# The order of the output products in the second half of a spectral and mixture kernel: in whole tiles four steps behind, or in single matmuls by a schedule that is three steps behind at both ends

## The chip, the cores and the metric

The kernel runs on one core of one Trainium2 chip. The metric is the device time of one execution in microseconds. A core has five engines with a queue of instructions each: PE (TensorE, matmuls; its weight loads have a row of their own, PEld), DVE (VectorE), ACT (ScalarE), POOL (GpSimd) and SP (SyncE, which issues the DMAs here). Each queue is worked off in the order in which the program wrote it; engines wait for each other through semaphores.

## The reference

Three layers in a row: a layer in the frequency domain over x [8, 3072, 256], a soft mixture of experts, and a two-layer network with a softmax-weighted activation and a layer norm over 24,576 tokens. The second half of the kernel computes what follows from the logits of the mixture to the end; the last layer is

```python
def _moe2_ref(x, w_in, w_out, g_ln):
    h = x @ w_in
    e = np.exp(h - np.max(h, axis=-1, keepdims=True))
    sm = e / (np.sum(e, axis=-1, keepdims=True) + 1e-09)
    solu = h * sm
    mu = np.mean(solu, axis=-1, keepdims=True)
    var = np.mean((solu - mu) ** 2, axis=-1, keepdims=True)
    ln = (solu - mu) / np.sqrt(var + 1e-06) * g_ln
    return (ln @ w_out).astype(np.float32)
```

Here x is the mixture's output. The kernel has multiplied the mixture's 32 slots with w_in beforehand, so that one product of a tile of mixture weights gives h at once, and it has folded g_ln and the mean's subtraction into w_out.

## The kernel before

The first half (some 637 us) computes the frequency layer, the mixture's weights and the slots. The second half is the function phase2. It cuts the 24,576 tokens into NI = 192 tiles of 128 tokens and runs a software pipeline over them, written out by hand: the loop at L1309 has a step i for every tile and six more, and each step issues a different stage of several tiles. No scheduler changes the order; what a step writes first stands first in its engine's queue. For tile t the stages are:

- hmat (L1059), in step t-3, on PE: two matmuls of 512 columns give h of the tile in PSUM ("hps", three buffers; the buffer comes free when umul of tile t-3 is done).
- rowmax (L1074), in step t-2, on DVE; expo (L1080), in step t-2, on ACT; umul (L1088), in step t-1, on DVE, the product of h and exp ("u").
- In step t-1 also, the transposition of u. For most tiles it is blocks (L1112): a DVE transpose of 32x32 blocks and four DMAs that move the blocks to their places ("t2"). For every eighth tile (turned, L1100: t % 8 == 6 and t < 172) it is turn (L1148) instead: eight transposes on PE into the tile's own hps, copied out by ACT. For the last two tiles (direct, L1097: 190 and 191) it is trans (L1123) in step t, eight transposes on PE into "pu", and direct_parts (L1137), where ACT writes the rounded half of u, and DVE the rest, half a tile at a time and by turns.
- vari (L1193), in step t, on ACT: the sum of squares.
- uhi (L1165), in step t+2: the transposed u rounded to the fast matmul format ("uh"), three quarters by ACT and one by POOL. ulo (L1177), in step t+2: the remainder ("ul"), in two halves on POOL (for tiles 188 and 189 the second half on DVE). In every fourth step the four small POOL instructions of rstd (L1224) stand between the two halves of ul.
- prod (L1200), in step t+4: the output product, 24 matmuls of 256 columns into a half of a PSUM bank ("po2"; two tiles share a bank, there are two banks): 16 with uh, then 8 with ul. A turned tile has 4 in plain float32 and 12 others.
- outp (L1239): ACT scales two tiles of the product into "osb", in every odd step i, for tiles i-7 and i-6; this frees their PSUM bank. Stores follow on SP.

The products of one tile are split in two places around a turned tile T: in step T-1 the first 16 of tile T-5 stand before turn(T) and the other 8 behind it, and in step T the first 12 of tile T-4 stand before hmat(T+3). In the first four steps six dummy matmuls ("idle", run_on) follow hmat.

Of the kernel before, what the change touches and what calls it, by code (L numbers as in the profile page):

```python
# [8 lines left out]
F32 = mybir.dt.float32  # L9
# [26 lines left out]
def kernel(  # L36
# [26 lines left out]
    B, N, D = x.shape  # L63
# [5 lines left out]
    NI = T // 128  # L69
# [18 lines left out]
    def mm(out, lhsT, rhs, start=True, stop=True):  # L88
        PE.matmul(out=out, lhsT=lhsT, rhs=rhs, start=start, stop=stop)  # L89

    def tp(out, in_, k=128):
        PE.transpose(out=out, in_=in_, identity=ident[0:k, 0:k])  # L92
# [813 lines left out]
    def phase2(p2: ExitStack, pw: ExitStack):  # L906
# [3 lines left out]
        gw = k_p.tile([128, 8, 2, D], F32R, name="gw")  # L910
# [13 lines left out]
        p = ExitStack()  # L924
# [5 lines left out]
        ps = pt.tile([128, 2, 32], F32, name="pslt", tag="pt")  # L930
# [85 lines left out]
        for fh in range(2):  # L1016
            n = 0
# [13 lines left out]
        def right(name, bufs, **k):  # L1031
            return p2.enter_context(tc.tile_pool(name=name, bufs=bufs, side="right", **k))

        f_p = right("f_p", 1)
        gwf = f_p.tile([128, 4, D], F32, name="gwf")
# [7 lines left out]
        po_p = right("po_p", 2, space=PSUM)  # L1043
        NG = NI // 4
        ctt, hps, et, ut, uht, stt, osb, pot = {}, {}, {}, {}, {}, {}, {}, {}
# [51 lines left out]
        def direct(i):  # L1097
            return i >= NI - 2

        def turned(i):  # L1100
            return i % 8 == 6 and i < NI - 20
# [21 lines left out]
        def trans(i):  # L1123
            if i >= NI or not direct(i):
                return
            ps = ph_p.tile([128, 8, 128], F32, name="pu", tag="hps")
            for c in range(8):
                tp(ps[:, c, :], ut[i][:, 128 * c:128 * c + 128])
            ut[i, 0] = ps
# [67 lines left out]
            sq = e_p.tile([128, DFF], F32, name="sq", tag="sq", bufs=1)  # L1197
            ACT.activation(out=sq, in_=ut.pop(i), func=AF.Square, bias=st[:, 2, k:k + 1], scale=-float(DFF), accum_out=st[:, 3, k:k + 1])  # L1198

        def prod(i, left=0):  # L1200
            if i < 0 or i >= NI:
                return
            if i not in pr_ops:
                uh, ul = uht.pop(i)
                if i % 2 == 0:
                    pot[i // 2, 0] = po_p.tile([128, 2, D], F32, name="po2", tag="po2")
                ps = pot[i // 2, 0][:, i % 2, :]
                if turned(i):
                    ops = [(uh[:, f, :].bitcast(F32), gwf[:, f, :]) for f in range(4)]
                    hi = [(f, ul[:, f - 4, :], ul[:, f, :]) for f in range(4, 8)]  # L1210
                else:
                    ops = []
                    hi = [(f, uh[:, f, :], ul[:, f, :]) for f in range(8)]
                for f, h, _ in hi:
                    ops += [(h, gw[:, f, 0, :]), (h, gw[:, f, 1, :])]
                ops += [(l, gw[:, f, 0, :]) for f, _, l in hi]
                pot[i] = ps
                pr_ops[i] = [(ps, a, b, n == 0, n == len(ops) - 1) for n, (a, b) in enumerate(ops)]
            ops = pr_ops[i]
            while len(ops) > left:  # L1220
                mm(*ops.pop(0))


        def rstd(i):  # L1224
            if i >= NI:
                return
            j, k = divmod(i, 4)
            if k < 3:
                return
            st = stt[j]  # L1230
            k = slice(0, 4)
            POOL.tensor_scalar(out=st[:, 1, k], in0=st[:, 1, k], scalar1=1e-9, scalar2=(1e-6 * float(DFF) ** 3) ** 0.5, op0=ALU.add, op1=ALU.mult)
            POOL.tensor_tensor(out=st[:, 1, k], in0=st[:, 1, k], in1=st[:, 1, k], op=ALU.mult)
            POOL.tensor_tensor(out=st[:, 3, k], in0=st[:, 3, k], in1=st[:, 1, k], op=ALU.add)
            POOL.tensor_tensor(out=st[:, 4, k], in0=st[:, 3, k], in1=mhalf[:, k], op=ALU.pow)

        o_todo, pr_ops = {}, {}

        def outp(i):  # L1239
            if i < 0 or i >= NI:  # L1240
# [22 lines left out]
        def run_on(n):  # L1263
            ps = po_p.tile([128, 128], F32, name="idle", tag="po2")
            for _ in range(n):
                mm(ps, ones, ones)
# [42 lines left out]
        for i in range(NI + 6):  # L1309
            j, k = divmod(i, 4)  # L1310
            if turned(i):
                prod(i - 4, 12)
            hmat(i + 3)
            if i < 4:
                run_on(6)
            trans(i)
            rowmax(i + 2)
            umul(i + 1)
            blocks(i + 1)
            store(i - 6)  # L1320
            late_c(i)
            last_c(i)
            if i % 2 == 1:
                outp(i - 7)
                outp(i - 6)
            if turned(i):
                expo(i + 2)
                vari(i)
            else:
                vari(i)  # L1330
                expo(i + 2)
            direct_parts(i)
            if i <= NI + 1:
                uhi(i - 2)
                ulo(i - 2, 0)
            rstd(i)
            if i <= NI + 1:
                ulo(i - 2, 1)
            if k == 1:
                pieces(j + 2)  # L1340
            if turned(i + 1):
                prod(i - 4, 8)
                turn(i + 1)
            prod(i - 4)
        while o_todo:
            store(min(o_todo))

# [143 lines left out]
```

## Time and profile before

| what | value |
|---|---|
| device time, median of 3 runs | 1326.49 us (1325.54 to 1326.93) |
| the profiled execution's own time | 1324.1 us |
| its span, first to last instruction | 1322.3 us |
| granted TensorE clock, mean over the span | 0.995 |
| PE busy, 11,040 matmuls | 1264.3 us, 96% of the span |
| PEld busy | 1113.9 us, 84% |
| DVE busy | 1161.5 us, 88% |
| POOL busy | 1013.4 us, 77% |
| ACT busy | 988.7 us, 75% |
| chain that ended last: share of PE, and of the output products alone | 72%, 37% |

The page's shares are means over both halves. The second half starts at about 637 us and is much denser than the first: in it PE, DVE, ACT and POOL are all busy for more than nine tenths of the time. So its limit is read step by step from the timeline, and from the chain of waits that ended last, which goes back from the last instruction to what released it.

### The profile page before, as it was taken

The page shows a single profiled execution, that of the slowest core. Times are in us where ns is not written, and L with a number is a line of the kernel's source. Part 1 is how long each engine was busy: PE and PEld are TensorE (multiplying, and loading weights), DVE is VectorE, ACT ScalarE, POOL GpSimd, SP SyncE. Part 2 cuts the span into 40 slices and gives each one's busy share as a digit, 9 for nine tenths or more (in the row PEclk, how much of TensorE's full clock was granted, in tenths as well). Part 3 has the DMA queues.
Part 4 walks back from the last instruction along what each step waited for, and adds up shares of the span by engine and source line. Part 5 has one row for each costly group of instructions (what it writes and reads, how often), then busy time and mean ns, then how long its engine had stood idle before and what let it go on. Part 6 is the DMA issues. An engine that isn't in the chain of part 4 may idle for free.

```text
span 1322.3 us, 30973 instructions
## 1 busy us (share of the span) xinstructions
PE 1264.3 (96%) x11040; PEld 1113.9 (84%) x11040; DVE 1161.5 (88%) x1564; ACT 988.7 (75%) x1830; POOL 1013.4 (77%) x1112
## 2 busy tenths in 40 slices
PE   5989999999999999998799999999999999999998
PEld 2768878776787878875599999999999999999998
DVE  1868898989898989765899999999999999999995
ACT  3445556555565665544599999999999999999996
POOL 0769686776869584442398999999999989999995
PEclk8999999999999999999999999999999999999999
DMA  8986465463828374349567778777877787777874
GB/s 265 271 233 186 127 168 168 124 196 96 240 68 240 80 208 157 113 125 354 126 165 176 200 190 204 199 180 188 198 196 199 179 217 196 193 200 178 202 187 123
DMA packets 181338, 241.79 MB, mean 183 GB/s; under 512 B 21984, under 2 KB 137056, under 8 KB 181184
## 3 DMA queue, kind: packets, MB, share of 16 engines
q1 hardware_dynamic: 180736, 238.62, 67.0%
q8 instruction: 88, 1.44, 0.5%
q10 hardware_dynamic: 448, 1.18, 0.3%
q14 instruction: 66, 0.54, 0.1%
HBM read 92.00 MB, written 59.11 MB: 114 GB/s over the span
## 4 chain that ended last, share of the span: by engine, by line
PE 72%; DVE 11%; POOL 5%; DMA 5%; issue 3%; ACT 2%; SPq 1%; DVEq 0%; ACTq 0%; POOLq 0%
PE po L89 37%; PE pb L89 7%; PE pm L89 6%; PE hps L89 6%; PE xps L89 5%; PE s L89 4%; PE pa L89 3%; PE sps L92 2%; DVE st L1078 2%; DVE u L1093 2%; PE hps L92 2%; DMA t<-tb 1%; DMA xc<-in_x_dram 1%; POOL x L229 1%; POOL x L225 1%
## 5 line engine op out<-in xcount | busy, mean ns | idle before, releaser
L1188 POOL TENSOR_TENSOR ul<-t,uh 128x512 fp32r<-128x512 f32 x336 | 431.1, 1301 | 43.3 <-ACT uh L1174 42.7
L89 PEld LDWEIGHTS po<-gw,uh 128*128 128x128 f32 x2736 | 347.4, 188 | 14.0
L89 PE MATMUL po<-gw,uh 128*128 128x256 f32 x2736 | 353.7, 280 | 0.0
L1078 DVE TENSOR_REDUCE st<-hps 128x1 f32<-128x1024 f32 x192 | 229.1, 1194 | 10.5 <-PE hps L89 10.5
L1093 DVE SCALAR_TENSOR_TENSOR u<-hps,e 128x1024 f32<-128x1024 f32 x192 | 232.1, 1209 | 0.5 <-ACT e L1085 0.3
L89 PE MATMUL po<-gw,ul 128*128 128x256 f32 x1620 | 228.1, 284 | 0.0
L1085 ACT ACTIVATE e<-hps,st 128x1024 f32<-128x1024 f32 x192 | 215.5, 1123 | 16.5 <-DVE st L1078 16.4
L1198 ACT ACTIVATE sq<-u,st 128x1024 f32<-128x1024 f32 x192 | 223.0, 1162 | 0.3 <-DVE u L1093 0.3
L1116 DVE STREAM_TRANSPOSE tb<-u 128x1024 f32<-128x1024 f32 x169 | 210.5, 1245 | 5.9
L349 POOL TENSOR_TENSOR s<-yb,s 128x512 f32<-128x512 f32 x95 | 124.7, 1312 | 112.3 <-DVE s L348 107.2
L89 PEld LDWEIGHTS po<-gw,ul 128*128 128x128 f32 x1620 | 206.1, 188 | 1.1
L1174 ACT ACTIVATE uh<-t 128x768 fp32r<-128x768 f32 x169 | 143.4, 849 | 0.0
L89 PEld LDWEIGHTS xps<-d_sb,apt 128*128 128x128 f32 x768 | 94.9, 194 | 56.6 <-issue 31.5
L89 PE MATMUL xps<-d_sb,apt 128*128 128x128 f32 x768 | 111.0, 288 | 13.7 <-DMA apt<-ad 10.1
L89 PE MATMUL hps<-gst,ct 128*128 128x512 f32 x338 | 106.2, 396 | 7.6 <-DVE u L1093 6.1
L252 ACT ACTIVATE asb<-s 128x1024 f32<-128x1024 f32 x56 | 57.6, 1028 | 72.5 <-PE s L89 67.1
L309 POOL TENSOR_TENSOR sl<-xsum,sh 128x256 fp32r<-128x256 f32 x93 | 76.5, 822 | 35.5 <-ACT sh L308 35.4
L225 POOL TENSOR_TENSOR x<-xc 112x512 f32<-112x512 f32 x56 | 73.5, 1313 | 37.9 <-DMA xc<-in_x_dram 37.9
L293 DVE TENSOR_TENSOR xsum<-xps,xi 128x256 f32<-128x256 f32 x96 | 39.6, 413 | 54.0 <-ACT xh L292 38.8
L1249 ACT ACTIVATE osb<-po,st 128x256 f32<-128x256 f32 x192 | 80.3, 476 | 8.3 <-PE po L89 4.7
L348 DVE TENSOR_SCALAR s<-yb 128x512 f32<-128x512 f32 x95 | 77.4, 815 | 3.7
L229 POOL TENSOR_TENSOR x<-xc 112x512 f32<-112x512 f32 x56 | 78.9, 1410 | 0.0
(211 smaller groups left out, 2389.3 us busy)
## 6 DMA issues: line engine op xcount, KB each, us to landing
t<-tb SPq DMA_DIRECT2D x676, 128.0 KB, 2.8
xc<-in_x_dram SPq DMA_DIRECT2D x128, 192.0 KB, 3.9
apt<-ad SPq DMA_DIRECT2D x96, 256.0 KB, 4.0
out_dram<-osb SPq DMA_DIRECT2D x47, 512.0 KB, 3.8
ad<-asb SPq DMA_DIRECT2D x112, 192.0 KB, 3.7
ct<-c_dram SPq DMA_DIRECT2D x96, 128.0 KB, 4.1
wt<-in_moe_w_dram SPq DMA_DIRECT2D x21, 512.0 KB, 9.1
ws<-in_moe_w_dram SPq DMA_DIRECT2D x22, 256.0 KB, 6.4
```

What stands on the lines that cost most here:

```text
L89: PE.matmul(out=out, lhsT=lhsT, rhs=rhs, start=start, stop=stop)
L225: POOL.tensor_tensor(out=z[0:112, 0], in0=t[:, 0], in1=t[:, 1], op=ALU.add)
L229: POOL.tensor_tensor(out=z[0:112, 1], in0=t[:, 0], in1=t[:, 1], op=ALU.subtract)
L349: POOL.tensor_tensor(out=s, in0=y, in1=s, op=ALU.subtract)
L1078: DVE.tensor_reduce(out=st[:, 0, k:k + 1], in_=hps[i], op=ALU.min, axis=AX.X)
L1085: ACT.activation(out=e, in_=hps[i], func=AF.Exp, bias=st[:, 0, k:k + 1], scale=-1.0, accum_out=st[:, 1, k:k + 1])
L1093: DVE.scalar_tensor_tensor(out=u, in0=hps[i] if turned(i) else hps.pop(i), scalar=1.0, in1=et.pop(i), op0=ALU.mult, op1=ALU.mult, accum_ou ...
L1116: DVE.transpose(out=t, in_=ut[i])
L1174: ACT.activation(out=w[:, 0:HA], in_=v[:, 0:HA], func=AF.Copy)
L1188: (DVE if n and i >= NI - 4 else POOL).tensor_tensor(out=ul[:, z, :].rearrange("p c (a j) -> p c a j", a=4), in0=v, in1=w.bitcast(F32), op ...
L1198: ACT.activation(out=sq, in_=ut.pop(i), func=AF.Square, bias=st[:, 2, k:k + 1], scale=-float(DFF), accum_out=st[:, 3, k:k + 1])
L1249: ACT.activation(out=o[:, k], in_=pot.pop(i), func=AF.Copy, scale=stt[j][:, 4, k:k + 1])
```

## The change

The function prod, which issued the products of one tile, is replaced by prods_to(p), which issues single matmuls until p tiles are done in all, p being a fraction of tiles. The schedule done(s) says how many are to be done at the end of step s: s - 2 at the start and from step 188 on (tile s-3 in step s, three behind), s - 3 from step 40 to step 172 (tile s-4, four behind, as before), and a slope between them, 1/32 tile a step from step 8 to step 40 and 1/16 tile a step from step 172 to step 188. The splits around a turned tile stay. For the two direct tiles the products of the step now stand ahead of trans instead of behind it. Nothing is computed differently, and the orders of ACT, DVE, POOL and SP stay as they were.

```diff
--- before.py
+++ after.py
@@ -1197,29 +1197,41 @@
             sq = e_p.tile([128, DFF], F32, name="sq", tag="sq", bufs=1)
             ACT.activation(out=sq, in_=ut.pop(i), func=AF.Square, bias=st[:, 2, k:k + 1], scale=-float(DFF), accum_out=st[:, 3, k:k + 1])
 
-        def prod(i, left=0):
-            if i < 0 or i >= NI:
-                return
-            if i not in pr_ops:
-                uh, ul = uht.pop(i)
-                if i % 2 == 0:
-                    pot[i // 2, 0] = po_p.tile([128, 2, D], F32, name="po2", tag="po2")
-                ps = pot[i // 2, 0][:, i % 2, :]
-                if turned(i):
-                    ops = [(uh[:, f, :].bitcast(F32), gwf[:, f, :]) for f in range(4)]
-                    hi = [(f, ul[:, f - 4, :], ul[:, f, :]) for f in range(4, 8)]
-                else:
-                    ops = []
-                    hi = [(f, uh[:, f, :], ul[:, f, :]) for f in range(8)]
-                for f, h, _ in hi:
-                    ops += [(h, gw[:, f, 0, :]), (h, gw[:, f, 1, :])]
-                ops += [(l, gw[:, f, 0, :]) for f, _, l in hi]
-                pot[i] = ps
-                pr_ops[i] = [(ps, a, b, n == 0, n == len(ops) - 1) for n, (a, b) in enumerate(ops)]
-            ops = pr_ops[i]
-            while len(ops) > left:
-                mm(*ops.pop(0))
-
+        def prod_ops(i):
+            uh, ul = uht.pop(i)
+            if i % 2 == 0:
+                pot[i // 2, 0] = po_p.tile([128, 2, D], F32, name="po2", tag="po2")
+            ps = pot[i // 2, 0][:, i % 2, :]
+            if turned(i):
+                ops = [(uh[:, f, :].bitcast(F32), gwf[:, f, :]) for f in range(4)]
+                hi = [(f, ul[:, f - 4, :], ul[:, f, :]) for f in range(4, 8)]
+            else:
+                ops = []
+                hi = [(f, uh[:, f, :], ul[:, f, :]) for f in range(8)]
+            for f, h, _ in hi:
+                ops += [(h, gw[:, f, 0, :]), (h, gw[:, f, 1, :])]
+            ops += [(l, gw[:, f, 0, :]) for f, _, l in hi]
+            pot[i] = ps
+            return [(ps, a, b, n == 0, n == len(ops) - 1) for n, (a, b) in enumerate(ops)]
+
+        cur = {"n": 0, "ops": [], "total": 0}
+
+        def prods_to(p):
+            while cur["n"] < min(p, NI):
+                if not cur["ops"]:
+                    cur["ops"] = prod_ops(cur["n"])
+                    cur["total"] = len(cur["ops"])
+                part = min(1.0, p - cur["n"])
+                left = cur["total"] - round(cur["total"] * part)
+                while len(cur["ops"]) > left:
+                    mm(*cur["ops"].pop(0))
+                if cur["ops"]:
+                    return
+                cur["n"] += 1
+
+        def done(s):
+            behind = min(max(s - 8, 0) / 32, 1.0, max(188 - s, 0) / 16)
+            return max(0.0, s - 2 - behind)
 
         def rstd(i):
             if i >= NI:
@@ -1234,7 +1246,7 @@
             POOL.tensor_tensor(out=st[:, 3, k], in0=st[:, 3, k], in1=st[:, 1, k], op=ALU.add)
             POOL.tensor_tensor(out=st[:, 4, k], in0=st[:, 3, k], in1=mhalf[:, k], op=ALU.pow)
 
-        o_todo, pr_ops = {}, {}
+        o_todo = {}
 
         def outp(i):
             if i < 0 or i >= NI:
@@ -1309,10 +1321,12 @@
         for i in range(NI + 6):
             j, k = divmod(i, 4)
             if turned(i):
-                prod(i - 4, 12)
+                prods_to((done(i - 1) + done(i)) / 2)
             hmat(i + 3)
             if i < 4:
                 run_on(6)
+            if direct(i):
+                prods_to(done(i))
             trans(i)
             rowmax(i + 2)
             umul(i + 1)
@@ -1339,9 +1353,9 @@
             if k == 1:
                 pieces(j + 2)
             if turned(i + 1):
-                prod(i - 4, 8)
+                prods_to(done(i) - 1 / 3)
                 turn(i + 1)
-            prod(i - 4)
+            prods_to(done(i))
         while o_todo:
             store(min(o_todo))
```

PE's order at the start, from the last dummy matmuls of step 3 on. In the kernel before (hps_8790, 8838 and 8902 are hmat of tiles 7, 8 and 9, uh_8750 and ul_8751 belong to tile 0, uh_8780 and ul_8781 to tile 1, uh_8807 to tile 2; the L92 row is turn of tile 6):

```order
L89 MATMUL idle_8759<-ones_64 128x128 x6
L89 MATMUL hps_8790<-gst_8381,ct_8570 128x512 x2
L89 MATMUL po2_8813<-gw_8380,uh_8750 128x256 x16
L89 MATMUL po2_8813<-gw_8380,ul_8751 128x256 x8
L89 MATMUL hps_8838<-gst_8381,ct_8575 128x512 x2
L89 MATMUL po2_8813<-gw_8380,uh_8780 128x256 x16
L92 MATMUL hps_8756<-ident_62,u_8842 128x128 x8
L89 MATMUL po2_8813<-gw_8380,ul_8781 128x256 x8
L89 MATMUL po2_8889<-gw_8380,uh_8807 128x256 x12
L89 MATMUL hps_8902<-gst_8381,ct_8575 128x512 x2
```

The same place in the changed kernel (hps_8815, 8862 and 8926 are hmat of tiles 7, 8 and 9; uh_8750 is tile 0, uh_8780 tile 1, uh_8832 and ul_8833 tile 2, uh_8872 tile 3):

```order
L89 MATMUL idle_8759<-ones_64 128x128 x6
L89 MATMUL po2_8790<-gw_8380,uh_8750 128x256 x16
L89 MATMUL po2_8790<-gw_8380,ul_8751 128x256 x8
L89 MATMUL hps_8815<-gst_8381,ct_8570 128x512 x2
L89 MATMUL po2_8790<-gw_8380,uh_8780 128x256 x16
L89 MATMUL po2_8790<-gw_8380,ul_8781 128x256 x8
L89 MATMUL hps_8862<-gst_8381,ct_8575 128x512 x2
L89 MATMUL po2_8878<-gw_8380,uh_8832 128x256 x16
L92 MATMUL hps_8756<-ident_62,u_8866 128x128 x8
L89 MATMUL po2_8878<-gw_8380,ul_8833 128x256 x8
L89 MATMUL po2_8878<-gw_8380,uh_8872 128x256 x12
L89 MATMUL hps_8926<-gst_8381,ct_8575 128x512 x2
```

One tile's 24 products have moved ahead of hmat of tile 7, and so every later hmat and the turn of tile 6 have one more tile's products ahead of them than before; between the turn and hmat of tile 9 there are 20 products in both.

PE's order at the end, from hmat of tile 191 on, in the kernel before (uh_17897 is tile 184, uh_17949 185, uh_18000 186, uh_18040 187, uh_18089 188; pu_18070 and pu_18120 are trans of tiles 190 and 191):

```order
L89 MATMUL hps_17983<-gstn_8621,ct_16944 128x512 x2
L89 MATMUL po2_18006<-gw_8380,uh_17897 128x256 x16
L89 MATMUL po2_18006<-gw_8380,ul_17898 128x256 x8
L89 MATMUL po2_18006<-gw_8380,uh_17949 128x256 x16
L89 MATMUL po2_18006<-gw_8380,ul_17950 128x256 x8
L92 MATMUL pu_18070<-ident_62,u_18032 128x128 x8
L89 MATMUL po2_18095<-gw_8380,uh_18000 128x256 x16
L89 MATMUL po2_18095<-gw_8380,ul_18001 128x256 x8
L92 MATMUL pu_18120<-ident_62,u_18079 128x128 x8
L89 MATMUL po2_18095<-gw_8380,uh_18040 128x256 x16
L89 MATMUL po2_18095<-gw_8380,ul_18041 128x256 x8
L89 MATMUL po2_18175<-gw_8380,uh_18089 128x256 x16
```

And in the changed kernel (ul_17919 is tile 184, uh_17970 185, uh_18023 186, uh_18064 187, uh_18138 188; pu_18119 and pu_18169 are trans of tiles 190 and 191; uh_18190, tile 189, follows the last row):

```order
L89 MATMUL hps_18006<-gstn_8621,ct_16944 128x512 x2
L89 MATMUL po2_17983<-gw_8380,ul_17919 128x256 x2
L89 MATMUL po2_17983<-gw_8380,uh_17970 128x256 x16
L89 MATMUL po2_17983<-gw_8380,ul_17971 128x256 x8
L89 MATMUL po2_18070<-gw_8380,uh_18023 128x256 x16
L89 MATMUL po2_18070<-gw_8380,ul_18024 128x256 x8
L89 MATMUL po2_18070<-gw_8380,uh_18064 128x256 x16
L89 MATMUL po2_18070<-gw_8380,ul_18065 128x256 x8
L92 MATMUL pu_18119<-ident_62,u_18056 128x128 x8
L89 MATMUL po2_18144<-gw_8380,uh_18138 128x256 x16
L89 MATMUL po2_18144<-gw_8380,ul_18139 128x256 x8
L92 MATMUL pu_18169<-ident_62,u_18128 128x128 x8
```

Tile 184 has moved ahead of hmat of tile 191, up to two matmuls; trans of 190 has moved from behind tile 185 to behind tile 187, and trans of 191 from behind tile 186 to behind tile 188.

ACT's order there, in the changed kernel (before it is the same, with other numbers; uh_18132 and uh_18184 are direct_parts of tiles 190 and 191, uh_18138 and uh_18190 are uhi of tiles 188 and 189, osb_18179<-po2_17983 is outp of tiles 184 and 185, which frees the bank for tile 188):

```order
L1198 ACTIVATE sq_18130,st_17903<-u_18056,st_17903 128x1024
L1144 ACTIVATE uh_18132<-pu_18119 128x512 x2
L1174 ACTIVATE uh_18138<-t2_17957 128x768
L1261 ACTIVATE osb_18179<-po2_17983,st_17696 128x256 x2
L1198 ACTIVATE sq_18182,st_17903<-u_18128,st_17903 128x1024
L1144 ACTIVATE uh_18184<-pu_18169 128x512 x2
L1174 ACTIVATE uh_18190<-t2_18014 128x768
```

Nothing moved here: uhi of tile 188 and the outp behind it stand behind the copies out of pu of tile 190, and uhi of tile 189 behind those of tile 191.

## Rows read from the trace of the kernel before

**Rows 1.** Busy time by stretch: columns are the engines' busy us (instructions), granted clock, DMA

```profile
640.00:645.00 5.00, 2.70 (x20) 2.26 (x19) 4.71 (x6) 3.53 (x7) 2.07 (x2) 1.00 0.00 0
...
900.00:950.00 50.00, 50.00 (x387) 48.30 (x386) 48.63 (x58) 48.87 (x88) 46.31 (x58) 1.00 0.74 184
```

**Rows 2.** The chain that ended last, 630 to 720 us: start, us, what

```profile
663.54 1.09 PE hps L92 x8
```

**Rows 3.** Timeline, PE in steps 4 and 9: start, us, what [idle before <-releaser]

```profile
656.47 0.73 PE L89 MATMUL hps<-gst,ct 128*128 128x512 f32 x2 [1.40 <-DVE u L1093]
...
675.31 0.62 PE L89 MATMUL hps<-gst,ct 128*128 128x512 f32 x2
675.77 2.04 PE L89 MATMUL po<-gw,uh 128*128 128x256 f32 x16
677.64 1.10 PE L89 MATMUL po<-gw,ul 128*128 128x256 f32 x8
678.58 0.62 PE L89 MATMUL hps<-gst,ct 128*128 128x512 f32 x2
```

**Rows 4.** Timeline, the second turned tile (14) on DVE and PE

```profile
689.86 1.21 DVE L1093 SCALAR_TENSOR_TENSOR u<-hps,e 128x1024 f32<-128x1024 f32 x1
...
691.14 1.09 PE L92 MATMUL hps<-ident,u 128*128 128x128 f32 x8
...
694.45 0.62 PE L89 MATMUL hps<-gst,ct 128*128 128x512 f32 x2
...
695.11 1.22 DVE L1078 TENSOR_REDUCE st<-hps 128x1 f32<-128x1024 f32 x1 [0.47 <-PE hps L89]
```

**Rows 5.** Timeline, second halves of ul of tiles 1, 5, 13, and osb of 0, 1

```profile
660.54 1.31 POOL L1188 TENSOR_TENSOR ul<-t,uh 128x512 fp32r<-128x512 f32 x1
...
668.56 0.83 ACT L1249 ACTIVATE osb<-po,st 128x256 f32<-128x256 f32 x2
...
675.63 1.30 POOL L1188 TENSOR_TENSOR ul<-t,uh 128x512 fp32r<-128x512 f32 x1
...
703.26 1.29 POOL L1188 TENSOR_TENSOR ul<-t,uh 128x512 fp32r<-128x512 f32 x1
```

**Rows 6.** Timeline, POOL at the end: ul of tiles 185 (second half), 186, 187

```profile
1296.58 1.30 POOL L1188 TENSOR_TENSOR ul<-t,uh 128x512 fp32r<-128x512 f32 x1
...
1298.18 2.52 POOL L1188 TENSOR_TENSOR ul<-t,uh 128x512 fp32r<-128x512 f32 x2
...
1300.99 2.55 POOL L1188 TENSOR_TENSOR ul<-t,uh 128x512 fp32r<-128x512 f32 x2
```

**Rows 7.** Timeline, PE and ACT from hmat of tile 190 to the product of 189

```profile
1288.94 0.71 PE L89 MATMUL hps<-gstn,ct 128*128 128x512 f32 x2
...
1292.48 0.71 PE L89 MATMUL hps<-gstn,ct 128*128 128x512 f32 x2
...
1299.55 1.06 PE L92 MATMUL pu<-ident,u 128*128 128x128 f32 x8 [0.67 <-DVE u L1093]
...
1301.40 0.60 ACT L1144 ACTIVATE uh<-pu 128x512 fp32r<-128x512 f32 x1
...
1304.05 0.83 ACT L1249 ACTIVATE osb<-po,st 128x256 f32<-128x256 f32 x2
...
1305.90 0.61 ACT L1144 ACTIVATE uh<-pu 128x512 fp32r<-128x512 f32 x1
...
1307.76 0.84 ACT L1174 ACTIVATE uh<-t 128x768 fp32r<-128x768 f32 x1
...
1309.81 2.04 PE L89 MATMUL po<-gw,uh 128*128 128x256 f32 x16
```

**Rows 8.** The first half: PE by stretch and in the timeline, clock at half and full

```profile
25.00:30.00 5.00, 1.74 (x8) 1.77 (x8) 0.00 (x0) 0.00 (x0) 0.00 (x0) 0.50 0.70 222
...
35.21 1.05 PE L89 MATMUL pb<-wc_l,xh 128*128 128x256 f32 x4
...
40.08 0.63 PE L89 MATMUL pb<-wc_h,xl 128*128 128x256 f32 x4
```

## The prediction

> **What bounds the kernel now.** I looked at the busy time by stretch first. In the first microseconds of the second half PE works for 2.70 of 5 us, while DVE works for 4.71: the pipeline fills, and DVE sets its pace. In the middle PE, DVE and ACT are all at 97% or more, so no share of busy time says which one is the limit [rows 1]. The chain of waits says PE: from the turn of tile 6 at 663.54 it runs through PE alone [rows 2]. Hence the obvious reading: before 663.54 PE has idle time (1.40 us ahead of hmat in step 4), after it none, and a product done earlier is time won.
>
> The timeline corrects that. PE's step is a pair for hmat, 0.46 us from start to start, then 16 products in 1.87 and 8 in 0.94: 0.117 us a product, 2.81 a tile, 3.27 a step [rows 3]. From turn to turn PE needs 27.60 us, 663.54 to 691.14, without a wait [rows 2, 4]. But the turn needs DVE's u of the same tile, and that ends at 689.86 + 1.21 = 691.07, just 0.07 ahead of the turn. From the turn to the next hmat stand 20 products in either kernel, 3.31 us, and DVE's rowmax follows at 695.11, its only wait in the cycle, 0.47 [rows 4]. So DVE and PE meet once in eight tiles within 0.07 us. A PE that arrives there earlier waits for u; one that arrives later delays DVE at once, and with it ACT and everything that follows.
>
> **The change, part by part.** Three behind means that tile t's products stand one step earlier. Their number stays, 24 a tile, and no DMA and no instruction of another queue moves. What they need is made in step t+2: uh by ACT, ul by POOL, and in every fourth step rstd stands between the halves of ul. Four behind, PE comes after all that. I go through the places where three behind, it doesn't.
>
> Start, tile 1. PE reaches hmat of tile 7 at most one tile's products less the idle time later than 656.47, at 657.9; with 0.46 and 20 products (2.34) it stands before the last four products of tile 1 at 660.7. POOL ends that half of ul at 660.54 + 1.31 = 661.85 [rows 3, 5]. PE waits 1.1 us. Then 4 products (0.47), hmat of tile 8 (0.46), 16 products (1.87): the turn of tile 6 starts at 664.65 instead of 663.54, and DVE is 1.1 us late. What hid these late halves was the fourth step.
>
> Tiles 4 and 5. The next cycle has 27.60 us of work less what the slope puts off by step 13, 5/32 tile or 0.44. Tile 4 needs the bank of tiles 0 and 1: ACT's osb ends at 668.56 + 0.83, now 1.1 later, at 670.5, and PE is there at 664.65 + 3.31 + 0.46 + 12 products (1.40) + 0.46 = 670.3, a wait of 0.2. Tile 5's second half ends at 675.63 + 1.30 + 1.1 = 678.0, and PE is there at 670.5 + 2.81 + 0.46 + 2.34 = 676.1, a wait of 1.9 [rows 5]. The turn of tile 14 comes at 664.65 + 27.60 - 0.44 + 2.1 = 693.9, against 691.14: 2.8 late.
>
> Tile 13. Its second half ends at 703.26 + 1.29 + 2.8 = 707.35. PE is there at 693.9 + 3.31 + 0.46 + 1.40 + two steps (6.54) + 0.46 + two products (0.23), less 0.26 put off, 706.0: a wait of 1.3. The turn of tile 22 comes 27.60 - 0.70 + 1.3 after that of 14, at 722.1 against 718.74: 3.4 late. From there on the slope takes 0.70 us a cycle off PE, more than such waits cost, so DVE sets the pace with its 27.60.
>
> Steps 40 to 172 read as before, cost nothing and give nothing back: PE's lead of up to a tile ends at each turn. At most it wins 0.07 in each of 20 cycles, 1.4 us; I take 0. So the start costs 3.4; its ends are -1.4 (no wait reaches DVE) and 4.4 (a further late half of the kind of tile 13, 1.0).
>
> Steps 172 to 188. There is no turned tile any more, and hmat follows DVE every 3.54 us (1288.94 to 1292.48) [rows 7], where PE needs 3.27. The slope adds 2.81/16 = 0.18 a step, which these 0.27 hide. Cost 0. If they didn't, hmat would come late, but it has most of a DVE step before rowmax asks for it.
>
> The tail. hmat of tile 191 comes with DVE, at 1292.48, and one tile less is left behind it: on paper 2.81 won. But PE is then at the second half of ul of tile 185 at 1292.48 + 0.46 + 22 products (2.57) = 1295.5, and POOL ends it at 1296.58 + 1.30 = 1297.88: a wait of 2.4, and tile 185 ends at 1298.35. Tile 186: ul is ready at 1298.18 + 2.52 = 1300.70, the last four products end at 1301.17. Tile 187: 1300.99 + 2.55 = 1303.54, and 1304.0 [rows 6]. So PE wins nothing here; POOL's queue gives the pace. Now the order tells: trans of 190, at 1299.55 before, comes behind tile 187, at 1304.0, and ends at 1305.1. ACT can copy from pu only then, not at 1301.40: 3.7 late. Queued behind these copies on ACT are uhi of tile 188 and the osb of tiles 184 and 185, which frees its bank; that ended at 1304.05 + 0.83, now 1308.6. PE's next work is tile 188, so PE stands idle from 1305.1 to 1308.6. Tile 188 ends at 1311.4, trans of 191 at 1312.5. ACT's copies, 1305.90 before, are 6.6 late, and uhi of tile 189 ends at 1307.76 + 0.84 + 6.6 = 1315.2; again PE stands idle, 2.7 us. Tile 189 starts at 1315.2 instead of 1309.81 [rows 7]. What follows waits for nothing but PE, so the end is 5.4 late, the 0.67 us that trans of 190 waited before included. Bounds: were POOL never late, trans of 190 would start at 1301.6, ACT be 1.3 late, tile 188 start at 1306.2, trans of 191 end at 1310.1, and tile 189 start 2.70 later (1305.90 to 1308.60), at 1312.8, 2.9 late; if the ul of tiles 188 and 189, with POOL and DVE at it together, are each 1 us late as well, 7.4.
>
> Sum: 3.4 + 0 + 0 + 5.4 = 8.8 us. The profiled execution took 1324.1 (span 1322.3), so 1332.9; the median is 2.4 above that execution, which makes 1335.3.
>
> A rule that speaks against the change. In the first half PE sat idle and then worked at a granted clock of 0.50, the lower of the two levels, where four products of 256 columns took 1.05 us against 0.63 at the full one [rows 8]; in the second half the clock was 1.00 even where PE worked 2.70 of 5 us [rows 1]. The Trainium skill ("TensorE: Matmul & The Clock Gate", section "Why this matters for your kernels") says that idle gaps between bursts of matmuls let the clock fall. The two idle times in the tail would be such gaps; by the rule the products behind them run at 1.2 GHz and the sum grows, by the trace alone they may as well stay at 2.4. I make it a rival.
>
> **The rivals.**
> - Faster: PE's stream is the real limit, as the chain has it; a tile done in idle time at the start takes 2.81 off, the vanished wait in the tail 0.67, nothing is late: 1323.0. For it: no wait of PE between 663.54 and 1299. Against: the times of ul, and u only 0.07 ahead of the turn. It decides if POOL's second halves of tiles 1 and 5 land before PE asks.
> - The start's delay is won back in the middle, only the tail costs: 1331.9.
> - Only the start costs, the tail's idle times swallow what was there anyway: 1329.9. Against it stands ACT's order.
> - Gains and waits cancel, or the few moved products reach nothing: 1326.5.
> - The clock falls in the tail's idle times: (1.05 - 0.63)/4 = 0.105 us more for each of 24 products, 2.5 a tile, for one or two tiles: 1337.8 to 1340.3, say 1339.
>
> **How the numbers follow.** Both costs, 1335.3: 0.60. Tail alone 0.14, start alone 0.05, clock 0.08, no change 0.05, faster 0.08. A measurement of this kernel tells changes above 0.2%, 2.7 us. Slower by more than that: 0.60 + 0.14 + 0.05 + 0.08 = 0.87; same 0.05; faster 0.08. The range starts at 1329, where the tail costs its least and the start nothing, and goes to 1339, with 7.4 for the tail and 4.4 for the start: it leaves out the two cases on the other side and a part of the clock's.
>
> **What would show it.** Right: the turns of tiles 6, 14 and 22 some 1, 3 and 3.4 us later than before, waits of PE's products for POOL's ul in steps 4 and 8, the distance of turns 27.60 in the middle, and in the last 20 us two idle times of PE of about 3.5 and 2.7 us that end with ACT's osb or uh. Wrong: no such waits on PE, a turn of tile 22 earlier than 718.7, a cycle below 27.5, or PE without a gap after trans of tile 190.

## The result and the profile after

The changed kernel takes 1336.94 us (median of 6 runs, 1333.46 to 1340.99), the kernel before, measured beside it, 1326.35 (6 runs, 1323.57 to 1327.91): a ratio of 1.0085 with an interval of 1.0062 to 1.0108, so 0.6 to 1.1% slower, 11.3 us by the ratio. The profiled execution took 1333.46 us, its span 1331.7.

The first half ends at a different time in each execution: the first hmat of the second half starts at 637.66 us in the profile of before and at 636.02 in that of after, and between 636.5 and 644.0 in the other profiles below. So I count from the first hmat. From there to the end of the span it is 684.64 us before and 695.68 after: 11.0 later in these two executions.

**The start.** PE's timeline of after (start us, us, what, in brackets the idle time and what ended it):

```profile
636.02 1.66 PE L89 MATMUL hps<-gst,ct 128*128 128x512 f32 x6 [1.42 <-DVE gst L1027]
...
660.22 0.73 PE L89 MATMUL po<-gw,ul 128*128 128x256 f32 x4 [1.14 <-POOL ul L1188]
663.13 1.03 PE L92 MATMUL hps<-ident,u 128*128 128x128 f32 x8
...
668.22 0.62 PE L89 MATMUL hps<-gst,ct 128*128 128x512 f32 x2
668.96 2.17 PE L89 MATMUL po<-gw,uh 128*128 128x256 f32 x16
...
676.48 0.73 PE L89 MATMUL po<-gw,ul 128*128 128x256 f32 x4 [1.60 <-POOL ul L1188]
692.41 1.04 PE L92 MATMUL hps<-ident,u 128*128 128x128 f32 x8
...
705.80 0.75 PE L89 MATMUL po<-gw,ul 128*128 128x256 f32 x4 [1.05 <-POOL ul L1188]
...
720.61 1.03 PE L92 MATMUL hps<-ident,u 128*128 128x128 f32 x8
...
734.01 0.74 PE L89 MATMUL po<-gw,ul 128*128 128x256 f32 x4 [0.37 <-POOL ul L1188]
```

And POOL's timeline of after, with the second half of ul of tile 1 behind the four instructions of rstd:

```profile
655.68 1.30 POOL L1188 TENSOR_TENSOR ul<-t,uh 128x512 fp32r<-128x512 f32 x1 [0.66 <-ACT uh L1174]
657.06 0.19 POOL L1244 TENSOR_SCALAR st<-st 128x4 f32<-128x4 f32 x1
...
657.89 1.03 POOL L1247 TENSOR_TENSOR st<-st,mhalf 128x4 f32<-128x4 f32 x1
658.89 1.27 POOL L1188 TENSOR_TENSOR ul<-t,uh 128x512 fp32r<-128x512 f32 x1
```

Before, PE had no wait in this place. Its 8 products with ul of tile 1 stood behind the turn of tile 6, and the second half had been ready since 661.85:

```profile
664.39 1.20 PE L89 MATMUL po<-gw,ul 128*128 128x256 f32 x8
```

The second halves that PE now waits for are those of [rows 5]. The half of tile 1 ends at 658.89 + 1.27 = 660.16, and PE's four products start at 660.22. The same stands at tiles 5 and 13, and for a last time, 0.37, at tile 29; ahead of tile 4, PE's products start 0.74 after the start of hmat instead of 0.46, for the bank: ACT's osb of tiles 0 and 1 ends at 668.91, and PE starts at 668.96. From the first hmat, the turns of tiles 6 and 14 were 25.88 and 53.48 us away before [rows 2, 4] and are 27.11 and 56.39 now; the turn of tile 22 is at 84.59 (before 81.08). So 1.2, 2.9 and 3.5 us late.

**The middle.** The waits of after, 700 to 850 us (engine, line, waited for: us, times, longest), and its busy time by stretch (columns as in [rows 1]):

```profile
DVE st L1078 <- PE hps L89: 2.9, 5, 1.1
PE po L89 <- POOL ul L1188: 1.4, 2, 1.1
```
```profile
900.00:950.00 50.00, 50.00 (x385) 48.23 (x384) 48.67 (x57) 48.85 (x88) 46.54 (x57) 1.00 0.76 187
```

DVE's one wait a cycle is still there, and the stretch from 900 to 950 is that of [rows 1] again. The last turn, of tile 166, is 3.4 us late (581.04 us after the first hmat, 577.66 before): over 18 cycles 0.1 us came back.

**The tail.** PE and ACT in the timeline of after, which answer to [rows 6, 7]:

```profile
1295.28 0.62 PE L89 MATMUL hps<-gstn,ct 128*128 128x512 f32 x2
...
1299.62 0.74 PE L89 MATMUL po<-gw,ul 128*128 128x256 f32 x4 [1.11 <-POOL ul L1188]
...
1305.92 1.04 PE L92 MATMUL pu<-ident,u 128*128 128x128 f32 x8
1307.05 0.60 ACT L1144 ACTIVATE uh<-pu 128x512 fp32r<-128x512 f32 x1 [3.81 <-PE pu L92]
...
1309.70 0.83 ACT L1261 ACTIVATE osb<-po,st 128x256 f32<-128x256 f32 x2
1310.59 3.67 PE L89 MATMUL po<-gw,uh 128*128 128x256 f32 x16 [3.63 <-ACT osb L1261]
...
1315.06 1.03 PE L92 MATMUL pu<-ident,u 128*128 128x128 f32 x8
1316.19 0.60 ACT L1144 ACTIVATE uh<-pu 128x512 fp32r<-128x512 f32 x1 [4.53 <-PE pu L92]
...
1318.92 2.17 PE L89 MATMUL po<-gw,uh 128*128 128x256 f32 x16 [2.83 <-ACT uh L1174]
```

PE and ACT work by turns: ACT waits 3.81 us for the transposes, PE 3.63 for what ACT does behind them, ACT again 4.53, PE again 2.83. And the 16 products behind the first idle time take 3.67 us, against 2.04 for the same 16 before [rows 7]. The busy time by stretch of after says why:

```profile
1307.00:1310.50 3.50, 0.00 (x0) 0.00 (x0) 1.99 (x3) 2.62 (x6) 0.61 (x1) 1.00 0.00 0
1310.50:1314.00 3.50, 3.41 (x16) 3.42 (x17) 1.20 (x1) 1.16 (x3) 1.46 (x2) 0.53 0.00 0
1316.00:1319.00 3.00, 0.17 (x2) 0.08 (x1) 1.43 (x3) 2.06 (x4) 0.00 (x0) 1.00 0.01 3
1319.00:1322.00 3.00, 3.00 (x25) 3.00 (x26) 0.65 (x1) 0.60 (x2) 2.67 (x5) 1.00 0.44 175
```

In the stretch behind the first idle time the granted clock is 0.53, mostly the lower of its two levels (1.2 GHz); behind the second it is 1.00 (2.4 GHz).

### The profile page after: what moved, and what is told of

Read it like the earlier page. It is cut to its first block, busy times and chain, and to the rows that moved or that the text cites. A ratio compares the mean times of both kernels' runs of the same rounds, so it can differ in the third digit from the quotient of the medians.

```text
span 1331.7 us, 30970 instructions
## 1 busy us (share of the span) xinstructions
PE 1266.0 (95%) x11040; PEld 1115.3 (84%) x11040; DVE 1162.7 (87%) x1564; ACT 988.5 (74%) x1830; POOL 1013.2 (76%) x1112
## 4 chain that ended last, share of the span: by engine, by line
PE 66%; DVE 11%; POOL 8%; issue 5%; DMA 5%; ACT 3%; SPq 2%; DVEq 0%; ACTq 0%; POOLq 0%
PE po L89 34%; PE pb L89 6%; PE pm L89 5%; PE hps L89 5%; PE xps L89 5%; PE s L89 4%; PE pa L89 3%; POOL x L229 2%; PE sps L92 1%; POOL ul L1188 1%; POOL x L225 1%; PE hps L92 1%; DVE u L1093 1%; DMA t<-tb 1%; DMA xc<-in_x_dram 1%
## 5 line engine op out<-in xcount | busy, mean ns | idle before, releaser
L89 PE MATMUL po<-gw,uh 128*128 128x256 f32 x2736 | 359.8, 281 | 6.6 <-ACT osb L1261 3.6
L1078 DVE TENSOR_REDUCE st<-hps 128x1 f32<-128x1024 f32 x192 | 229.1, 1194 | 13.5 <-PE hps L89 13.5
L89 PE MATMUL po<-gw,ul 128*128 128x256 f32 x1620 | 231.8, 284 | 5.9 <-POOL ul L1188 5.9
L89 PEld LDWEIGHTS po<-gw,ul 128*128 128x128 f32 x1620 | 208.9, 189 | 9.9 <-POOL ul L1188 7.1
```

The lines of the kernel that those rows point to most:

```text
L1078: DVE.tensor_reduce(out=st[:, 0, k:k + 1], in_=hps[i], op=ALU.min, axis=AX.X)
```

## The experiments

All were measured beside the kernel before, whose medians in the three sets were 1325.49, 1326.66 and 1326.09 us; "above before" is reckoned by the ratio. The table sets the profiled executions side by side. "Late" is how much later than before the last turn comes, counted from the first hmat; "whole" the same for the end of the span; the tail is the difference. "16 products" are those behind the first and the second long idle time of PE in the tail, or how long PE's idle times are there where there are no such two.

| kernel | ratio to before, interval | late | whole | tail | 16 products, us |
|---|---|---|---|---|---|
| changed | 1.0085, 1.0062 to 1.0108 | 3.4 | 11.0 | 7.7 | 3.67, 2.17 |
| start alone | 1.0033, 1.0020 to 1.0046 | 3.6 | 3.9 | 0.2 | none over 0.7 |
| end alone | 1.0075, 1.0055 to 1.0095 | 0.1 | 10.0 | 9.9 | 3.78, 3.52 |
| trans first | 1.0023, 1.0008 to 1.0037 | 3.7 | 3.8 | 0.1 | none over 1.2 |
| first idle time filled | 1.0094, 1.0075 to 1.0112 | 3.6 | 13.5 | 9.9 | 2.17, 3.14 |
| both filled | 1.0066, 1.0047 to 1.0085 | 3.6 | 9.8 | 6.1 | 2.14, 2.15 |
| changed, rstd behind | 1.0072, 1.0050 to 1.0095 | 0.3 | 9.3 | 9.1 | 2.59, 3.68 |
| start, rstd behind | 0.9995, 0.9983 to 1.0008 | 0.3 | 0.5 | 0.2 | none over 0.7 |
| before, rstd behind | 1.0006, 0.9991 to 1.0021 | 0.2 | 0.4 | 0.2 | none over 0.7 |
| before, fewer between | 0.9994, 0.9981 to 1.0008 | -1.2 | -1.6 | -0.4 | none over 0.7 |
| fewer between | 0.9964, 0.9951 to 0.9977 | -2.8 | -3.1 | -0.3 | none over 0.7 |
| fewer between, no end | 0.9969, 0.9954 to 0.9984 | -2.8 | -3.2 | -0.3 | none over 0.7 |

**Start alone.** Three behind at first, four to the end; the products of the direct tiles behind trans again.

```diff
-            behind = min(max(s - 8, 0) / 32, 1.0, max(188 - s, 0) / 16)
+            behind = min(max(s - 8, 0) / 32, 1.0)
-            if direct(i):
-                prods_to(done(i))
```

> Three behind at the start with the slope to four, the end as in the kernel before (four behind to the last tile, the transposes of the direct tiles ahead of the step's products). Theory (late halves of ul make PE late at a turn, a late turn makes DVE late, nothing is won back): turn of tile 22 some 3.4 us later after the start of the second half than before, and that distance kept to the last turn; time 1326.4 + 3.4 = 1329.8. Rival 1 (the start's lateness is won back, only the tail costs): 1326.4, last turn as early as before. Rival 2 (PE's stream is the limit, a tile done early is won): 1323.6.

Measured 1329.96 us (1325.83 to 1334.35, 12 runs), 4.4 above before by the ratio. The turns of tiles 6, 14 and 22 come 27.12, 56.40 and 84.58 us after the first hmat, as in the changed kernel. The start's delay is real, and the middle does not win it back.

**End alone.** Four behind from the start, three behind at the end, products of the direct tiles ahead of trans.

```diff
-            behind = min(max(s - 8, 0) / 32, 1.0, max(188 - s, 0) / 16)
+            behind = min(1.0, max(188 - s, 0) / 16)
```

> Four behind from the start to step 172, then the slope to three behind and the products ahead of the transposes of the direct tiles, as in the changed kernel. Theory (PE and ACT take turns over tiles 188 and 189, and the clock falls in PE's first idle time): last turn as before, tile 189's product some 7.4 us later, 5.4 from the order and about 2 from the clock; time 1333.8, and a wide spread between runs. Rival 1 (the start is the main cost, the tail is small): 1327 or less. Rival 2 (one tile less behind hmat of 191 is won): 1323.5.

Measured 1335.52 us (1331.25 to 1339.95, 6 runs), 9.9 above before, more than the expected 1333.8. PE's timeline of this kernel in the tail shows where the rest went:

```profile
1304.73 1.03 PE L92 MATMUL pu<-ident,u 128*128 128x128 f32 x8
1309.40 3.78 PE L89 MATMUL po<-gw,uh 128*128 128x256 f32 x16 [3.63 <-ACT osb L1261]
1312.98 1.91 PE L89 MATMUL po<-gw,ul 128*128 128x256 f32 x8
...
1318.65 3.52 PE L89 MATMUL po<-gw,uh 128*128 128x256 f32 x16 [2.83 <-ACT uh L1174]
```

The idle times are those of the changed kernel to the hundredth, 3.63 and 2.83 us, but here the products are slow behind both, and the first time the 8 with ul too. Before, 16 and 8 products read 2.04 and 1.10 us [rows 3].

**Trans first.** The changed kernel without its special case for the direct tiles.

```diff
-            if direct(i):
-                prods_to(done(i))
```

> The changed kernel with one edit: for the direct tiles the step's products stand behind the transposes again; the schedule is three behind at both ends. Theory (the alternation with ACT comes from the place of the transposes, not from three behind): no idle time of PE above 1 us in the last 25 us, granted clock 1.00 there, the tail within 1 us of before, time 1326.4 + 3.4 = 1329.8. Rival (three behind itself costs the tail, because POOL is late with tiles 185 to 187): still 1332 or more.

Measured 1328.51 us (1325.85 to 1333.29, 12 runs), 3.0 above before. PE's timeline of this kernel in the tail:

```profile
1304.86 1.03 PE L92 MATMUL pu<-ident,u 128*128 128x128 f32 x8
1305.65 2.15 PE L89 MATMUL po<-gw,uh 128*128 128x256 f32 x16
...
1308.59 1.03 PE L92 MATMUL pu<-ident,u 128*128 128x128 f32 x8
...
1313.24 2.14 PE L89 MATMUL po<-gw,uh 128*128 128x256 f32 x16 [0.58 <-ACT uh L1174]
```

With the transposes of 190 ahead of tile 187, ACT copies while PE works on that tile, and both long idle times are gone. What is left is the start's 3.7. So the tail's cost hangs on the place of the transposes; three behind at the end costs nothing by itself. One idle time stays, of 1.12 us at 1301.44, for POOL's ul of tile 185; none above 1 was expected.

**First idle time filled.** 13 products of constants, which nobody reads, between trans of 190 and tile 188, and 10 between tiles 189 and 190, the latter not in an idle time. The function fill, not shown here, issues them into a buffer of hps; the profile counts two matmuls for each.

```diff
+            if i == NI - 1:
+                fill(13)
             if direct(i):
                 prods_to(done(i))
+            if i == NI:
+                fill(10)
```

> The changed kernel with 13 dummy matmuls of the idle kind (some 3.25 us) between the transposes of tile 190 and the product of tile 188, and 10 (2.5 us) between the product of tile 189 and that of 190, where they are to cost their own time. Theory of the clock (PE's idle time of 3.6 us let the clock fall to half for 3.5 us): the 16 first products of tile 188 take 1.9 us instead of 3.5, the tail is 1.6 shorter there and 2.5 longer by the second fill, time 1337.8 against 1336.9, with a spread between runs as small as before's (4 us or less). Rival (the products were slow for another reason, such as their inputs): they stay at 3.5 us and the time rises by 2.5 to 1339.4.

Measured 1337.87 us (1335.72 to 1342.48, 6 runs). As a test of the clock's price this failed: the fillers kept the clock behind the first idle time (2.17 us for the 16), but behind the second, unfilled one they took 3.14, where the changed kernel kept the full clock; and the ten in the other place are work on the path. The spread of the runs did not shrink either. That the time met the 1337.8 of the theory does not bear it out: by the theory the tail is 7.7 - 1.6 + 2.5 = 8.6 us, and the profile has 9.9.

**Both filled.** The second filler moved into the second idle time.

```diff
+            if i == NI - 1:
+                fill(13)
             if direct(i):
                 prods_to(done(i))
             trans(i)
+            if i == NI - 1:
+                fill(10)
```

> The changed kernel with products of constants into an unused bank in both idle times of PE in the tail: 13 of 128 columns between trans of tile 190 and the products of tile 188, and 10 between trans of tile 191 and those of tile 189. They add work that nobody reads. Theory (the order costs 5.5 us, and a fall of the clock behind the idle times the rest): the granted clock stays at 1.00 from 1305 us to the end, the 16 products behind either idle time take 1.9 to 2.2 us, PE starts tile 189 at the time that ACT's copies allow, and the time is 2 us below the changed kernel's, 1335. Rival (the clock is not worth anything, because only idle time ends later): 1337, as the changed kernel. A second rival: the fillers themselves put off tile 188 and 189: 1338 or more.

Measured 1334.45 us (1332.14 to 1338.18, 6 runs), 8.8 above before. PE's timeline of this kernel:

```profile
1313.05 3.07 PE L89 MATMUL fill<-ones 128*128 128x128 f32 x26
1316.85 2.14 PE L89 MATMUL po<-gw,uh 128*128 128x256 f32 x16 [0.73 <-ACT osb L1261]
...
1320.64 2.40 PE L89 MATMUL fill<-ones 128*128 128x128 f32 x20
1323.64 2.15 PE L89 MATMUL po<-gw,uh 128*128 128x256 f32 x16 [0.60 <-ACT uh L1174]
```

Added work that nobody reads made the tail of the profiled execution shorter, 6.1 us against 7.7, and both groups of 16 run at the full clock. That parts the two prices: order about 6, the clock the rest. The other profiles agree. From the start of tile 188's products to that of trans of 191, and from the start of tile 189's to that of tile 190's, PE takes 2.92 and 2.98 us here, 4.47 and 2.87 in the changed kernel, 5.28 and 4.30 with the end alone, 2.96 and 6.62 with the first idle time filled (its ten fillers included), and 4.09 and 4.46 in the changed kernel with rstd behind, which comes next. Added to 6.1, the differences give tails of 7.6, 9.8, 9.8 and 8.8 us, where 7.7, 9.9, 9.9 and 9.1 were measured. By the medians the gain over the changed kernel is 2.5 us; there the two intervals overlap, so it is the trace that shows it.

**The changed kernel, rstd behind.**

```diff
-            rstd(i)
             if i <= NI + 1:
                 ulo(i - 2, 1)
+            rstd(i)
```

> The changed kernel, but rstd of a group of four tiles is put on GpSimd's queue behind the second half of ul of the tile two steps back, no longer ahead of it. Theory (the start is lost because PE asks for the second halves of ul of tiles 1, 5 and 13 that rstd had put off): these halves end about 1.9 us earlier, PE's waits for ul in the start (1.1 and 1.6 us in the changed kernel) go, and what stays of the 3.5 us is the bank of tile 4 (0.2 us): the turns of tiles 6, 14 and 22 at most 0.5 us later than before, counted from the first hmat; the tail is as in the changed kernel, so 3.4 us less than it, about 1333.5. Rival (the start is lost to something else, the banks or uh): the turns stay 1.2, 2.9 and 3.5 us late, 1336.9.

Measured 1335.06 us (1331.56 to 1339.16, 6 runs), 9.5 above before. POOL's timeline of this kernel, tile 1:

```profile
656.19 2.55 POOL L1188 TENSOR_TENSOR ul<-t,uh 128x512 fp32r<-128x512 f32 x2 [0.66 <-ACT uh L1174]
658.82 0.19 POOL L1244 TENSOR_SCALAR st<-st 128x4 f32<-128x4 f32 x1
```

Both halves now stand together, PE's waits for them in the start are gone, and the turns of tiles 6, 14 and 22 come 25.88, 53.56 and 81.11 us after the first hmat: within 0.1 of before. So what the start costs three behind is rstd's place, as the theory has it. The time fell by 1.8 us only, not 3.4: in this kernel's profile the products behind both idle times are slow (2.59 and 3.68 us), behind one in the changed kernel's. In these two executions the last turn comes 3.1 us earlier and the tail is 1.4 longer; how much of the 1.6 that is missing in the time is this, six runs can't say.

**Start alone, rstd behind.** The edits of the start alone and of rstd behind together.

> Only the start of the change (three behind at first, four from step 40 to the end), with rstd behind the second half of ul. Theory: the start's waits go (turn of tile 22 at most 0.5 us late, against 3.5), and nothing is won either, because DVE's u stands at the turn: 1326.4 to 1327. Rival of the faster side (PE's stream is the limit, a tile done in idle time at the start is time won): turn of tile 22 about 2.5 us early, 1323.6. Rival of the other side (the start's cost has another cause than rstd's place): 1329.9, as with the start alone.

Measured 1325.51 us (1323.06 to 1327.97, 12 runs): no change. A tile's products done in idle time at the start are worth nothing, for PE then waits for DVE's u at the turns until the slope has used up its lead. The third and the fourth turn in PE's timeline of this kernel:

```profile
717.64 1.09 PE L92 MATMUL hps<-ident,u 128*128 128x128 f32 x8 [0.56 <-DVE u L1093]
...
745.24 1.09 PE L92 MATMUL hps<-ident,u 128*128 128x128 f32 x8 [0.51 <-DVE u L1093]
```

**Before, rstd behind.** The same move in the kernel before, as a control.

> The kernel before with nothing but rstd put behind the second half of ul. Theory: in the kernel before PE is four tiles behind and asks for these halves a step after they are there, so an earlier ul ends no wait: turns as before (25.88, 53.48, 81.08 us after the first hmat), 1326.5. Rival (rstd behind is itself a gain, which would then be in the version with fewer products between as well): 1325 or less. Rival of the other side (rstd later holds up the output): 1328 or more.

Measured 1325.66 us (1322.11 to 1329.17, 12 runs): no change. Four behind, the late halves were hidden.

**Fewer between.** A version meant to win. In the changed kernel with trans first and rstd behind, 4 products instead of 12 stand between a turn's last 8 and the next hmat, and the lag grows over 48 steps. The edits of those two are not shown again.

```diff
-            behind = min(max(s - 8, 0) / 32, 1.0, max(188 - s, 0) / 16)
+            behind = min(max(s - 8, 0) / 48, 1.0, max(188 - s, 0) / 16)
-                prods_to((done(i - 1) + done(i)) / 2)
+                prods_to(done(i - 1) + (done(i) - done(i - 1)) / 6)
```

> A version meant to win: the changed kernel with trans ahead of the products as before, rstd behind the second half of ul, the lag growing over 48 steps, and 4 products instead of 12 between a turned tile's turn (with its 8) and the next hmat. Theory: DVE's only wait of a cycle, 0.47 us for hmat after a turn, goes for as long as PE is ahead (about six cycles, each given back to PE's lead), 2 to 3 us in all; start at most 0.5 us; the tail as with trans first, about 1 us better than before: 1323 to 1324. Rival (PE, not DVE, sets the cycle, so an earlier hmat only moves the products behind it to a later turn): cycle stays 27.6, 1325.5 to 1326.5.

Measured 1321.42 us (1320.69 to 1324.99, 12 runs): 0.2 to 0.5% faster than before, 4.8 us by the ratio; in the profiled executions it is 3.1. PE's turns in the timeline of this kernel (tiles 30, 38, 46, and two of the later ones), and of DVE the wait that is left there:

```profile
746.35 1.04 PE L92 MATMUL hps<-ident,u 128*128 128x128 f32 x8
773.51 1.03 PE L92 MATMUL hps<-ident,u 128*128 128x128 f32 x8
800.59 1.07 PE L92 MATMUL hps<-ident,u 128*128 128x128 f32 x8
...
937.70 1.03 PE L92 MATMUL hps<-ident,u 128*128 128x128 f32 x8
...
945.78 1.22 DVE L1093 SCALAR_TENSOR_TENSOR u<-hps,e 128x1024 f32<-128x1024 f32 x1 [0.36 <-ACT e L1085]
...
965.20 1.03 PE L92 MATMUL hps<-ident,u 128*128 128x128 f32 x8
```

The first two cycles take 27.89 and 27.42 us. From then on, while PE's lead lasts, a cycle takes 27.1 to 27.2 us, since DVE has no wait for hmat any more. Then the lead is spent, PE sets the pace with 27.51, and DVE waits 0.36 for ACT's e instead. The place of hmat turns PE's lead into time; the start alone with rstd behind had the lead, and no use for it.

**Before, fewer between.**

```diff
-                prod(i - 4, 12)
+                prod(i - 4, 20)
```

> The kernel before with 4 instead of 12 products between the turn's 8 and the next hmat, four tiles behind throughout. It parts the two halves of what the version with fewer products between won (4.8 us). Theory: DVE's wait of 0.47 us a cycle goes, but PE has no lead to pay for it, so PE sets the cycle with its own 27.51 us, as that version did after its sixth cycle, instead of 27.59: 20 x 0.08 = 1.6 us, 1325. Rival (the earlier hmat alone was the gain, the lead not needed): cycle 27.1, 10 us, 1317. Rival (no gain without the lead at all): 27.59, 1326.5.

Measured 1324.46 us (1319.83 to 1328.84, 11 runs), ratio 0.9994 with an interval of 0.9981 to 1.0008: by time it can't be told from no change, nor from the 1.6 us expected. The trace bears the theory out: turns 27.51 us apart from the second on (one cycle 27.76), the last one 1.2 us early and the end of the span 1.6. So in the trace the earlier hmat alone gives about half of the 3.1 us that the version with fewer products between wins there, and the other half needs the lead.

**Fewer between, no end.** Four behind to the end.

```diff
-            behind = min(max(s - 8, 0) / 48, 1.0, max(188 - s, 0) / 16)
+            behind = min(max(s - 8, 0) / 48, 1.0)
```

> The version with fewer products between, but four tiles behind to the end as in the kernel before, so that only the start's lead and the place of hmat are left of it. Theory (the lead of one tile, spent over six cycles, is the gain): last turn 574.9 us after the first hmat, 2.8 before that of the kernel before, and a tail as there: 1322.5 to 1323.5, at most 1 us above the version with the end's lag. Rival (a good part of the gain is from the shorter end): 1325 to 1326.

Measured 1321.34 us (1318.73 to 1326.91, 12 runs), a little better than expected, and the same as with the end. By the trace its gain is 3.2 us: about half is the place of hmat, which gives 1.6 without a lead, and the rest is the start's lead, spent over some cycles. The end's part of the change is worth nothing even when it does no harm.

## Why the prediction was right, and where it was not

The direction, both places and the kind of waits in them were as forecast, and 1336.9 lies 1.6 above the 1335.3 and in the range. The cost itself was forecast smaller than it is: 8.8 us, where the traces have 11.0 and the ratio 11.3. The tail is the term that was too small.

- **Start, 3.4.** Waits of 1.1, 0.2, 1.9 and 1.3 us were forecast for tiles 1, 4, 5 and 13; 1.14, 0.28 (0.74 less 0.46), 1.60 and 1.05 were measured, with 0.37 more at tile 29, which the sum did not have. Turns late by 1.1, 2.8 and 3.4 were forecast, by 1.2, 2.9 and 3.5 measured. The kernel with rstd behind shows the cause.
- **Middle, 0.** DVE and PE do meet at each turn, though 27.60 is not what PE needs, as the prediction reads it: without DVE's wait for hmat PE runs at 27.51 (before, fewer between), and DVE at 27.1 to 27.2 while PE is ahead (fewer between). 27.60 is the time of the loop through both, from u over the turn, 20 products and hmat to rowmax. 0.1 us came back, and the kernel with the start alone is as late at the last turn as at the third.
- **Slope at the end, 0.** It puts hmat of tile 191 later (1.1 us by the timelines, beyond the turns' 3.4), so the 0.27 us a step did not hide the slope, as the prediction has it, and PE's wait for ul of tile 185 is 1.11 us, not 2.4. But DVE's rowmax does not wait for that hmat: with trans first the tail is as long as before.
- **Tail, 5.4: mis-sized.** Idle times of 3.5 and 2.7 us, ended by osb and uh, were forecast, and 3.63 and 2.83 were measured. Tile 189 starts 7.4 us late in after, with the start's 3.4 taken off, and 5.9 late in the kernel with both idle times filled. So the step on the order of PE and ACT was 0.5 short, and the other 1.5 is the clock's: the step that failed is the one that ran the 24 products of tile 188 at the full rate. The clock was among the rivals, as a case beside the forecast, at 2.5 us a tile; it is a term that adds to it, of 1.6 us here (3.67 against 2.04 for the 16 products). In the profiles it is between 0.6 and 1.7 for a group of 16, and up to 0.8 for the 8 behind it; of the three profiles with both idle times unfilled one has one slow group and two have two. With it the sum is 3.4 + 5.9 + 1.6 = 10.9, where 11.0 was measured. The range's upper bound also has a tail of 7.4 us, but for ul of tiles 188 and 189 being late. PE waits for neither, so that this bound meets the measured tail is luck.

The Trainium skill ("TensorE: Matmul & The Clock Gate", section "Why this matters for your kernels") says that idle gaps of PE between bursts of matmuls, from a certain length on, take the clock back to half. The traces agree, though not each time: behind 2.83 us of idle time the clock was 1.00 in the changed kernel, and the same 2.83 us left 16 products at 3.52 us with the end alone. Why it differs between them, no run here settles.

The faster case (1323.0) fell with the start alone and rstd behind: its condition, that POOL's second halves land before PE asks, is met there, and the time is that of before. What it lacked was a place where DVE could use PE's lead.

## What to carry to other kernels

Where two engines meet at a fixed point of each cycle, work that one of them does early is worth nothing until the other's wait there is taken away; work that comes late is paid at once. Before a consumer is moved nearer to its producer, look what else stands in the producer's queue between the parts it needs (here four small instructions, 1.8 us from 657.06 to 658.89), and price an idle time that a new order opens on PE together with the products behind it, which may run at half the clock.

## What the runs showed of the hardware

- PE at a lowered clock behind idle times of 2.77 to 3.63 us, in six of the seven unfilled ones in the tails (granted clock 0.50 to 0.81 over the 16 products behind them); behind the seventh, 2.83 us in the changed kernel, it was 1.00, and 2.83 us is also the idle time of two of the six.
- Filling both idle times with products that nobody reads kept the clock at 1.00 and made the tail shorter (6.1 against 7.7 us); with only the first filled, the clock fell behind the second (16 products in 3.14 us).
- The first half's end varies by 8 us between executions of these kernels (first hmat from 636.0 to 644.0 us after the span's start) while the second half repeats within 0.5 us of before in the two kernels that made no difference (whole 0.4 and 0.5 in the table). Times of single runs therefore hide changes of 0.2%, which show in the trace once counted from the first hmat.
